# A conditional last group: one conditional with two copies of what follows, or two conditionals around the result ahead of it

## The chip, the cores and the metric

The kernel runs on one core of a Trainium2 chip. The core has a matrix engine (TensorE, here PE, with its weight loads as PEld), a vector engine (DVE), a scalar engine (ACT), GpSimd (POOL) and SyncE (SP). Each engine has a sequencer that runs its own list of instructions in order; the engines wait for each other through semaphores. In this kernel SP starts nearly all the transfers from HBM, and POOL the scatters of result rows. The metric is the device time of one execution in microseconds (us), told as the median of the runs.

## The reference

Attention in chunks, and behind it a mixture of experts with one expert per token. Cut to what is computed:

```python
# attention: B, H, S, D = 8, 8, 576, 64, in chunks of 64
scores = (1/8) * q_c @ k_c.T              # per chunk, 64 x 64
attn = softmax(scores)
x = (attn @ v_c) -> (4608, 512)           # tokens x (heads * 64)

# router: 8 experts, cosine similarity
xn, en = x / (|x| + 1e-6), emb / (|emb| + 1e-6)
logits = xn @ en.T / tau
expert = argmax(logits);  gate = max(softmax(logits))

# experts: 512 -> 1024 -> 512, each token through its own
out[t] = gate[t] * (relu(x[t] @ w1[expert[t]]) @ w2[expert[t]])
```

All in float32. How many tokens go to which expert is known only when the router has run, on the device.

## The kernel before

**Two halves.** The first half (up to about 195 us) does the attention in 36 tiles of 128 tokens, the router, and writes each token's row to a place in DRAM (`spots`) that is sorted by expert. `groups()` then counts: each expert's tokens are cut into groups of 64, an expert's last group being partly empty. `places()` works out, for every group, the row it starts at, its expert, and whether weights must be loaded. `second` is a column of `keep`, 1 on the partitions 64 to 127 and 0 below.

**Steps and pairs.** The second half goes through the groups two at a time: a step j takes one group from the front of the sorted list and one from its end, one on each half of the 128 partitions (index s = 0, 1). 36 pairs (j = 0 to 35) are always there; `LEAST` is 36. For a pair, SP loads the tokens (`load_x`, into `xin` and `spot`), DVE turns them (`turn_xb`), PE multiplies by w1 into `h`, ACT applies the relu, DVE turns the hidden values (`hT`), PE multiplies by w2 into `y_ps` (`result`, L408), ACT scales by the gate into `y` (L420), and POOL scatters 128 rows to `out` (L427). The hidden layer of pair j + 1 is computed ahead of the result of pair j, so PE has work while ACT and DVE turn the hidden values. The order is written out by hand: each engine runs its instructions as the program has them.

**Weights on condition.** `load_w2` and `load_late` issue a 2 MB transfer per half with a flag: `load_when` (L169 to L174) reads an expert number and a flag into registers of SP, and the transfer moves data only if the flag is set. `take_next` (L290) copies new w1 weights into place inside a `tc.If` when the expert changes.

**What follows the 36 pairs.** The number of groups may be odd, and there may be more than 72. `n_odd` and `n_steps` are read into registers of all five engines (L132). Then:

- If there is an odd group (`tc.If`, L1211), `step_alone(36, before_last)` does it as a step of its own with one group, that is 64 tokens. Its hidden layer comes first, then `before_last()` with the result of pair 35 and a load of w2, then its own result. This one is laid out differently: the 64 tokens fill the 128 partitions twice, once for each half of the 512 output columns, so the result is 128x256 and goes into a tile S. `at2` (L425) is the row number doubled, plus `second`, and the scatter goes to half rows of `out`. Then `more(37)`.
- Else (L1217), `load_x(39)`, `before_last()`, the loads, and `more(37)` once more.

`more(j)` is a nest: inside a `tc.If` on the number of steps (L1206) stands a `step_alone(j)` and then `more(j + 1)`, up to j = 44. So the program holds these eight steps twice, once in each branch.

**What a conditional becomes.** Every engine that takes part has a compare-and-branch. Behind the true block stands, out of line, a false block that raises the engine's semaphores by what the true block would have raised them (the make-up block), so that later waits count right. In the program before, the blocks stand in this order: the odd branch with its eight nested steps, their make-up blocks (the innermost first), the other branch with its eight steps, their make-up blocks, and the end. In the order of the instructions of the two built programs, PE has 7261 before and 6420 after, SP 2170 and 1846, DVE 2180 and 2053, ACT 1180 and 1056, POOL 1432 and 1362.

**At the end** (L1247) SP waits for all the semaphores and drains, then all five engines meet at a barrier, which POOL gathers and releases.

Of the kernel before, what the change touches and what calls it, by code (L numbers as in the profile page):

```python
# [1 line left out]

# [7 lines left out]
FP32 = mybir.dt.float32  # L10
BF16 = mybir.dt.bfloat16
I32 = mybir.dt.int32
AF = mybir.ActivationFunctionType
ALU = mybir.AluOpType
# [11 lines left out]
def kernel(  # L26
# [88 lines left out]

    n_steps = keep.tile([1, 1], I32, name="n_steps")
    n_odd = keep.tile([1, 1], I32, name="n_odd")
    second = keep.tile([P, 1], FP32, name="second")
    bp = ctx.enter_context(tc.tile_pool(name="blk", bufs=2))

    def whole(w):
# [36 lines left out]
    def load_x(j):  # L158
        rows = []
        for s in range(2 if j != LEAST else 1):  # L160
            row = number(src_row[of_step(s, j)], SPARE, ENG.SP)
            rows.append(spots[ds(row, G), :])
        load_rows(j, rows)
# [12 lines left out]
    def load_w2(j):  # L176
        for s in range(2):
            at = of_step(s, j)
            load_when(w2_sb[s][buf_of(j)], w2_rows, eblk[at], fresh[at])
# [8 lines left out]
    def load_late(j):  # L188
        for s in range(2 if j != LEAST else 1):
            at = of_step(s, j)  # L190
            load_when(next_w1[s], w1_rows, eblk[at], swap[at])
# [14 lines left out]
    def gates(j):  # L206
        for _ in gate_parts(j):
            pass
# [188 lines left out]
        swap_next()  # L397
        turn(1)

    def result(j, ps_y):  # L400
        d = mo.pop(j)
        ps = ps_y.tile([P, D], FP32, tag="y", name="y_ps")
        one_group = j == LEAST
        w = D // 2 if one_group else D
        for c in range(KF):
            for r in range(P // Q):
                t0, s, d0 = (r % 2, 0, w * (r // 2)) if one_group else (r, r // 2, 0)
                nc.tensor.matmul(  # L408
                    ps[Q * r : Q * r + Q, 0:w],
                    lhsT=d["hT"][:, c, Q * t0 : Q * t0 + Q],  # L410
                    rhs=w2_sb[s][buf_of(j)][:, c, d0 : d0 + w],
                    start=(c == 0),
                    stop=(c == KF - 1),
                )
        if one_group:
            S = late_p.tile([P, 3, KD // 2, 2, Q], FP32, tag="S", name="S", bufs=2)
            y = S.rearrange("p a c b i -> p (a c b i)")
        else:
            y = bp.tile([P, D], FP32, tag="y", name="y", bufs=1)
        nc.scalar.activation(y[:, 0:w], ps[:, 0:w], AF.Copy, scale=gate_of.pop(j))  # L420
        to, at, bound = out, spot[:, j % SPOTS, TOK : TOK + 1].bitcast(I32), N - 1
        if one_group:

            at2 = bp.tile([P, 1], I32, tag="at2", name="at2")
            nc.vector.tensor_scalar(at2, at, 2.0, second, ALU.mult, ALU.add)  # L425
            to, at, bound = out.rearrange("n (s d) -> (n s) d", s=2), at2, 2 * N - 1
        ins = nc.gpsimd.indirect_dma_start(  # L427
            out=to,
            out_offset=bass.IndirectOffsetOnAxis(ap=at, axis=0),
            in_=y[:, 0:w],  # L430
            in_offset=None,
            bounds_check=bound,
            oob_is_err=False,
        )
        tc.declare_no_dep(ins.ins, group="rows", reason="blocks hold different tokens")
        tc.add_to_no_dep_group("rows", ins.ins)
# [8 lines left out]
    with (  # L445
# [417 lines left out]
        def groups():  # L863


            half = 0.5 - 0.5 / G
            n_g = one.tile([P, E], FP32, name="n_g")
            nc.vector.tensor_scalar(
                nb[:, 1 : E + 1], rt_ps[:, 3, 0], 1.0 / G, half, ALU.mult, ALU.add
            )  # L870
            nc.vector.tensor_scalar(
                nb[:, 1 : E + 1], nb[:, 1 : E + 1], ROUND, ROUND, ALU.add, ALU.subtract
            )
            left = one.tile([P, E], FP32, name="left")
            nc.vector.tensor_tensor(left, nb[:, 1 : E + 1], done, ALU.subtract)
            nc.vector.tensor_tensor_scan(n_g, ones, left, 0.0, ALU.mult, ALU.add)
            nc.vector.tensor_scalar(off, n_g[:, E - 1 : E], -1.0, second, ALU.add, ALU.mult)
            nc.vector.tensor_tensor(first, n_g, left, ALU.subtract)
            nc.vector.tensor_scalar(mid, n_g[:, E - 1 : E], 0.5, -0.25, ALU.mult, ALU.add)
            nc.vector.tensor_scalar(mid, mid, ROUND, ROUND, ALU.add, ALU.subtract)  # L880
            nc.vector.scalar_tensor_tensor(
                out=odd, in0=mid, scalar=-2.0, in1=n_g[:, E - 1 : E], op0=ALU.mult, op1=ALU.add
            )
            nc.vector.tensor_tensor(ahead, odd, first_s, ALU.mult)


            nc.vector.tensor_scalar(
                jump[:, 0], nb[:, 0:E], -float(G), float(R), ALU.mult, ALU.add
            )
            nc.vector.scalar_tensor_tensor(  # L890
                out=jump[:, 0], in0=done, scalar=float(G), in1=jump[:, 0], op0=ALU.mult, op1=ALU.add
            )
# [234 lines left out]
    with (  # L1127
        tc.tile_pool(name="ps_h", bufs=1, space=PSUM, reuse_waits="tile") as ps_h,
        tc.tile_pool(name="ps_y", bufs=2, space=PSUM, reuse_waits="tile") as ps_y,
    ):  # L1130
        H_PS = [P, G // Q, KF * Q]

        def hidden_plain(j, w1, behind_it=None):
            for s in range(2 if j != LEAST else 1):
                ps = bank(ps_h, H_PS)
                for b in range(G // Q):
                    hidden_part(j, s, b, w1, None, None, ps)
                if behind_it is not None:
                    behind_it(s)

        def first_parts():
            for g in first_gates:
                next(g, None)

        first_parts()
        for j in range(LEAST - 1):
            n = j + 2

            def turn_next():
                if n < LEAST:  # L1150
                    turn_xb(n)
                    if n + XBUF < NJ:
                        load_x(n + XBUF)
                    add_x(n)

            def swap_next():
                if NE <= n < LEAST:
                    take_next(n)

            if j == 0:  # L1160
                first_parts()
                add_up(0, None, TS)
                first_parts()
            elif j == 1:
                turn_next()
                add_up(1, None, TS)
                hidden_plain(2, w1_sb, lambda s: add_up(s, None, ("T3",)))
            else:
                gate = gate_parts(n) if n < LEAST else iter(())
                hidden_fast(j + 1, ps_h, gate, turn_next, swap_next)  # L1170

            result(j, ps_y)
            if NE <= next_of(j) < NJ:
                load_w2(next_of(j))
            if NE - 1 <= n < LEAST - 1:
                load_behind(n)
            elif n == LEAST - 1:
                load_late(LEAST)

        steps = number(n_steps, NST, ENG.PE, ENG.DVE, ENG.Activation, ENG.Pool, ENG.SP)  # L1180

        odd_one = number(n_odd, 1, ENG.PE, ENG.DVE, ENG.Activation, ENG.Pool, ENG.SP)

        def before_last():
            result(LEAST - 1, ps_y)
            load_w2(LEAST + 1)

        def step_alone(j, between=None):
            turn_xb(j)
            if j + XBUF < NJ:  # L1190
                load_x(j + XBUF)
            gates(j)
            hidden_plain(j, next_w1)
            if j + 1 < NJ:
                load_late(j + 1)
            if between is not None:
                between()
            result(j, ps_y)
            if j + 2 < NJ:
                load_w2(j + 2)  # L1200

        def more(j):
            if j == NJ:
                return

            with tc.If(steps > j - NE - 1):  # L1206
                step_alone(j)
                more(j + 1)

        had, had_mo, had_gate = dict(xin), dict(mo), dict(gate_of)  # L1210
        with tc.If(odd_one > 0) as if_odd:  # L1211
            step_alone(LEAST, before_last)
            more(LEAST + 1)
        for now, then in ((xin, had), (mo, had_mo), (gate_of, had_gate)):
            now.clear()
            now.update(then)
        with if_odd.Else():  # L1217
            del xin[LEAST]
            load_x(LEAST + XBUF)
            before_last()  # L1220
            load_w2(LEAST + 2)
            load_late(LEAST + 1)
            more(LEAST + 1)


# [26 lines left out]
```

## Time and profile before

| what | value |
|---|---|
| time, median of 3 runs | 657.39 us (654.38 to 658.06) |
| time of the profiled execution | 657.75 us |
| its span, first to last instruction | 656.0 us |
| mean granted TensorE clock | 0.993 |
| PE, busy | 617.0 us (94%) |
| ACT, DVE, POOL, busy | 429.7, 425.3, 183.9 us |
| last matmul ends at about | 645 us |
| bytes moved by DMA, mean rate | 112.68 MB, 172 GB/s |

Times in the profile are us from the start of the span. A row of the timeline gives start, duration, engine, line, operation, what it writes and reads, the count, and in brackets how long the engine had been idle before it and what ended that. A line view gives, per engine and operation, the count, the shortest, median and longest duration in ns, and the first and last start in us; a q behind the engine's name means that its sequencer alone is at work. A row of waits gives the engine, tile and line that waited, what it waited for, the total in us, how many times, and the longest. In such a view taken branches and compares are both called COMPARE_BRANCH.

### The profile page before, as it was taken

How to read it: one execution, taken by the hardware profiler on the slowest of the kernel's cores; microseconds unless marked ns; L12 is line 12 of the kernel's file. 1: busy time of each engine (PE TensorE's matmuls, PEld its weight loads, DVE VectorE, ACT ScalarE, POOL GpSimd, SP SyncE). 2: the span in 40 equal slices, each digit the busy share in tenths (PEclk: the TensorE clock that was granted, in tenths of full speed). 3: DMA queues.
4: the chain of work that ended last, by engine and by line, in shares of the span. 5: the costliest groups of instructions: out<-in, count | busy, mean ns of one | idle time of the engine just before them, and what ended most of it. 6: DMA issues, size and time to landing. Idle time of an engine off the chain costs nothing. (4 is left out here: it accounts for less than half of the span.)

```text
span 656.0 us, 24867 instructions
## 1 busy us (share of the span) xinstructions
PE 617.0 (94%) x9744; PEld 344.5 (53%) x9744; DVE 425.3 (65%) x1140; ACT 429.7 (66%) x758; POOL 183.9 (28%) x262
## 2 busy tenths in 40 slices
PE   6899989898898989999999999999999999999993
PEld 5778878775443435445444544665444444444431
DVE  4878888786697446647784566979546666654430
ACT  4767767674316757767676767776777777676650
POOL 7759897762410100003020002303010021000101
PEclk9999999999998999999999999999999999999998
DMA  9999999988528711112787111776821116311111
GB/s 259 302 253 276 275 293 283 333 280 299 220 64 304 285 41 40 46 39 72 285 316 265 53 44 43 292 302 236 341 62 44 47 39 217 129 39 35 51 32 36
DMA packets 91696, 112.68 MB, mean 172 GB/s; under 512 B 49260, under 2 KB 69484, under 8 KB 91560
## 3 DMA queue, kind: packets, MB, share of 16 engines
q1 hardware_dynamic: 79512, 71.99, 34.0%
q0 software_dynamic: 12016, 38.89, 17.5%
q8 instruction: 81, 1.33, 0.8%
q14 instruction: 55, 0.45, 0.2%
q10 hardware_dynamic: 32, 0.02, 0.0%
HBM read 334.71 MB, written 22.69 MB: 545 GB/s over the span
## 5 line engine op out<-in xcount | busy, mean ns | idle before, releaser
L408 PE MATMUL y_ps<-w,hT 128*32 128x512 f32 (+1 forms) x2368 | 278.0, 587 | 2.9 <-DMA w<-in_moe_w_dram 2.9
L356 ACT ACTIVATE h<-C 64x256 f32<-64x256 f32 x264 | 179.4, 679 | 69.9 <-DVE C L369 67.1
L408 PEld LDWEIGHTS y_ps<-w,hT 128*32 128x32 f32 x2368 | 91.2, 110 | 155.4 <-issue 136.0
L427 POOL DMA_INDIRECT out_dram<-y,spot x36 | 37.5, 1042 | 392.4 <-ACT y L420 301.6
L337 PE MATMUL h<-w,S 128*32 128x256 f32 x1056 | 108.4, 382 | 1.8 <-DVE w L286 1.8
L337 PE MATMUL h<-sums,xbT 128*32 128x256 f32 x1056 | 109.0, 383 | 0.5 <-DVEq L294 0.5
L369 DVE TENSOR_TENSOR C<-C,h 128x256 f32<-128x256 f32 x231 | 96.0, 416 | 11.2 <-PE h L337 4.4
L363 DVE STREAM_TRANSPOSE hT<-h 128x512 f32<-128x512 f32 x66 | 46.7, 708 | 55.2 <-ACT h L356 54.5
L337 PE MATMUL h<-w,xbT 128*32 128x256 f32 x1056 | 82.3, 379 | 0.0
L222 DVE TENSOR_SCALAR rn<-rn 128x1 f32<-128x1 f32 x37 | 5.6, 151 | 87.6 <-ACT rn L219 87.6
L337 PEld LDWEIGHTS h<-w,S 128*32 128x32 f32 x1056 | 49.3, 110 | 24.2 <-DVE w L286 1.5
L337 PEld LDWEIGHTS h<-sums,xbT 128*32 128x32 f32 x1056 | 49.4, 111 | 23.2 <-DVEq L294 1.4
L337 PEld LDWEIGHTS h<-w,xbT 128*32 128x32 f32 x1056 | 43.6, 110 | 31.6 <-issue 9.0
L420 ACT ACTIVATE y<-y_ps,gate 128x512 f32<-128x512 f32 x36 | 24.8, 688 | 50.6 <-issue 44.7
L337 PE MATMUL h<-sums,S 128*32 128x256 f32 x528 | 53.4, 379 | 0.0
L816 POOL DMA_INDIRECT spots<-xr,dest x36 | 37.4, 1039 | 28.0 <-DVE dest L781 9.8
L198 DVE STREAM_TRANSPOSE xbT<-xin 128x256 f32<-128x256 f32 x73 | 44.4, 646 | 0.5 <-DVE hT L363 0.5
L219 ACT ACT_TABLE_LOAD x34 | 43.6, 1283 | 0.9 <-issue 0.4
L226 ACT ACT_TABLE_LOAD x34 | 43.6, 1283 | 0.6
L698 ACT COPY xT<-tr 128x512 f32<-128x512 f32 x36 | 21.1, 586 | 32.3 <-PE tr L696 32.3
L586 POOL DMA_DIRECT2D kx<-in_k_dram x36 | 31.9, 888 | 13.4 <-PE tr L612 12.6
L586 POOL DMA_DIRECT2D qx<-in_q_dram x40 | 34.5, 865 | 0.7 <-PE tr L612 0.6
(204 smaller groups left out, 802.2 us busy)
## 6 DMA issues: line engine op xcount, KB each, us to landing
w<-in_moe_w_dram SPq DMA_DIRECT2D x74, 2048.0 KB
next_w<-in_moe_w_dram SPq DMA_DIRECT2D x67, 2048.0 KB
xin<-spots SPq DMA_DIRECT2D x158, 64.0 KB
qx<-in_q_dram POOLq DMA_DIRECT2D x32, 256.0 KB, 5.9
v<-in_v_dram SPq DMA_DIRECT2D x58, 128.0 KB
kx<-in_k_dram POOLq DMA_DIRECT2D x28, 256.0 KB, 4.6
spots<-blank SPq DMA_DIRECT2D x9, 144.0 KB
spot<-spots SPq DMA_DIRECT2D x80, 4.0 KB
```

The costliest lines, as they stand in the source:

```text
L198: nc.vector.transpose(xT[:, :, cols].rearrange("p c (b i) -> p b c i", i=Q), t[:, s * (D // 2) : (s + 1) * (D // 2)].rearrange("p (b i c) ...
L219: nc.scalar.activation(rn, spot[:, j % SPOTS, SQ : SQ + 1], AF.Sqrt)
L226: nc.scalar.activation(sh, sh, AF.Exp, accum_out=gate)
L337: nc.tensor.matmul(ps[t0 : t0 + Q], lhsT=a[:, c, s], rhs=w[:, r], start=c == 0, stop=c == KD // 2 - 1,)
L356: nc.scalar.activation(h[b][G * v : G * v + G, s].rearrange("p (k i) -> p k i", i=Q), x[G * s : G * s + G].rearrange("p (i k) -> p k i", i=Q),
L363: nc.vector.transpose(hT.rearrange("p k (s b i) -> p b s k i", b=2, i=Q)[:, b], h[b].rearrange("p s (k i) -> p s k i", i=Q),)
L369: nc.vector.tensor_tensor(out, a, b, op)
L408: nc.tensor.matmul(ps[Q * r : Q * r + Q, 0:w], lhsT=d["hT"][:, c, Q * t0 : Q * t0 + Q], rhs=w2_sb[s][buf_of(j)][:, c, d0 : d0 + w], start= ...
L420: nc.scalar.activation(y[:, 0:w], ps[:, 0:w], AF.Copy, scale=gate_of.pop(j))
L427: ins = nc.gpsimd.indirect_dma_start(out=to, out_offset=bass.IndirectOffsetOnAxis(ap=at, axis=0), in_=y[:, 0:w], in_offset=None, bounds_ch ...
L586: eng.dma_start(out=x[done : done + n], in_=src[b, :, s : s + n, :].rearrange("h p d -> p h d"),)
L816: ins = nc.gpsimd.indirect_dma_start(out=spots, out_offset=bass.IndirectOffsetOnAxis(ap=at, axis=0), in_=m, in_offset=None, bounds_check=S ...
```

## The change

The conditional on the odd group becomes two, with the result of pair 35 between them and outside of both.

- First conditional: `turn_xb`, `gates` and the hidden layer of step 36.
- Outside: `load_x(39)`, a tile S that POOL sets to zero, the result of pair 35, `load_w2(37)`, `load_late(37)`.
- Second conditional: the matmuls of step 36's result and its scaling into S (`scaled`).
- Outside: `at2` and the scatter of S, then `load_w2(38)` and `more(37)`, which is now written once.

Since the scatter runs also when there is no odd group, `half_row` replaces `second` in `at2`: for an even count it is larger by 2N, which puts every row number out of bounds, and the scatter drops such rows. It is worked out in `groups()` by two more DVE operations. `second` and `half_row` are two columns of one tile. `result` is split into `scaled` and `scatter`, with the conditional as an argument.

```diff
-    second = keep.tile([P, 1], FP32, name="second")
+    by_half = keep.tile([P, 2], FP32, name="by_half")
+    second, half_row = by_half[:, 0:1], by_half[:, 1:2]
...
-    def result(j, ps_y):
+    def result(j, ps_y, y=None, when=nullcontext):
+        if y is None:
+            y = bp.tile([P, D], FP32, tag="y", name="y", bufs=1)
+        with when():
+            scaled(j, ps_y, y)
+        scatter(j, y)
+
+    def scaled(j, ps_y, y):
         d = mo.pop(j)
...
-        if one_group:
-            S = late_p.tile([P, 3, KD // 2, 2, Q], FP32, tag="S", name="S", bufs=2)
-            y = S.rearrange("p a c b i -> p (a c b i)")
-        else:
-            y = bp.tile([P, D], FP32, tag="y", name="y", bufs=1)
-        nc.scalar.activation(y[:, 0:w], ps[:, 0:w], AF.Copy, scale=gate_of.pop(j))
+        nc.scalar.activation(y, ps[:, 0:w], AF.Copy, scale=gate_of.pop(j))
+
+    def scatter(j, y):
         to, at, bound = out, spot[:, j % SPOTS, TOK : TOK + 1].bitcast(I32), N - 1
-        if one_group:
+        if j == LEAST:
             at2 = bp.tile([P, 1], I32, tag="at2", name="at2")
-            nc.vector.tensor_scalar(at2, at, 2.0, second, ALU.mult, ALU.add)
+            nc.vector.tensor_scalar(at2, at, 2.0, half_row, ALU.mult, ALU.add)
...
             nc.vector.tensor_tensor(ahead, odd, first_s, ALU.mult)
+            nc.vector.tensor_scalar(half_row, odd, -2.0 * N, 2.0 * N, ALU.mult, ALU.add)
+            nc.vector.tensor_tensor(half_row, half_row, second, ALU.add)
...
-        had, had_mo, had_gate = dict(xin), dict(mo), dict(gate_of)
-        with tc.If(odd_one > 0) as if_odd:
-            step_alone(LEAST, before_last)
-            more(LEAST + 1)
-        for now, then in ((xin, had), (mo, had_mo), (gate_of, had_gate)):
-            now.clear()
-            now.update(then)
-        with if_odd.Else():
-            del xin[LEAST]
-            load_x(LEAST + XBUF)
-            before_last()
-            load_w2(LEAST + 2)
-            load_late(LEAST + 1)
-            more(LEAST + 1)
+        def when_odd():
+            return tc.If(odd_one > 0)
+
+        with when_odd():
+            turn_xb(LEAST)
+            gates(LEAST)
+            hidden_plain(LEAST, next_w1)
+        load_x(LEAST + XBUF)
+        S = late_p.tile([P, 3, KD // 2, 2, Q], FP32, tag="S", name="S", bufs=2)
+        y_odd = S.rearrange("p a c b i -> p (a c b i)")[:, 0 : D // 2]
+        nc.gpsimd.memset(y_odd, 0.0)
+        result(LEAST - 1, ps_y)
+        load_w2(LEAST + 1)
+        load_late(LEAST + 1)
+        result(LEAST, ps_y, y_odd, when_odd)
+        load_w2(LEAST + 2)
+        more(LEAST + 1)
```

More of the change, by code (lines that the diff above doesn't have):

```diff
@@ L1 @@
-from contextlib import ExitStack
+from contextlib import ExitStack, nullcontext
 import concourse.bass as bass
@@ L429, in result @@
             out_offset=bass.IndirectOffsetOnAxis(ap=at, axis=0),
-            in_=y[:, 0:w],
+            in_=y,
             in_offset=None,
@@ L1182, with step_alone @@
         odd_one = number(n_odd, 1, ENG.PE, ENG.DVE, ENG.Activation, ENG.Pool, ENG.SP)
[L1184 to L1188, printed above, removed]
+        def step_alone(j):
             turn_xb(j)
@@ L1195, in step_alone @@
                 load_late(j + 1)
-            if between is not None:
-                between()
             result(j, ps_y)
```

## The prediction

> **What bounds the kernel now.** I read the page's busy times first, then the stretch that the diff touches (the timeline from 641 us), then, because little engine work is left there, the sequencers' own records of the lines that branch and end the program (line views, which give count, shortest, median and longest duration in ns, and first and last start).
>
> ```profile
> PE 617.0 (94%) x9744; PEld 344.5 (53%) x9744; DVE 425.3 (65%) x1140; ACT 429.7 (66%) x758; POOL 183.9 (28%) x262
> ```
>
> PE sets the pace to 645 us. Everything that the diff edits at the end stands in the last 27 us; of the 656.0 us span, the last 11 have no matmul. The timeline there:
>
> ```profile
> 641.66 0.69 ACT L420 ACTIVATE y<-y_ps,gate 128x512 f32<-128x512 f32 x1 [5.62 <-issue]
> 642.61 4.05 SPq L172 DMA_DIRECT2D w<-in_moe_w_dram  x4
> 642.63 0.97 POOL L427 DMA_INDIRECT out_dram<-y,spot  x1 [9.35 <-ACT y L420]
> 645.07 0.47 ACT L420 ACTIVATE S<-y_ps,gate 128x256 f32<-128x256 f32 x1 [2.72 <-PE y_ps L408]
> 645.82 0.97 POOL L427 DMA_INDIRECT out_dram<-S,at  x1 [2.22 <-ACTq L1206]
> ```
>
> Two readings decide much. First, the half-width result into S runs: **with these inputs there is an odd group**, so the kernel before takes the first of its two copies, and no further step follows. The second copy, which the change deletes, costs no time now. Second, the order at the end is PE, then ACT 645.07 to 645.54, then the scatter at 645.82. What comes after it is seen in the sequencers alone:
>
> ```profile
> L1206 SPq EVENT_SEMAPHORE  x9: 17/17/17, 650.3 to 650.9; - x9
> L1206 PEldq COMPARE_BRANCH  x2: 3417/3983/4549, 643.3 to 647.0; - x2
> L1206 SPq COMPARE_BRANCH  x2: 38/44/50, 646.7 to 651.0; - x2
> L1206 POOLq EVENT_SEMAPHORE  x2: 43/43/43, 646.8 to 650.0; - x2
> L1206 POOLq INC_SWDGE_SEM  x1: 1026/1026/1026, 650.1 to 650.1; - x1
> L1206 POOLq COMPARE_BRANCH  x1: 38/38/38, 651.1 to 651.1; - x1
> ```
>
> ```profile
> L1247 SPq EVENT_SEMAPHORE  x12: 28/28/28, 653.7 to 654.4; - x12
> L1247 SPq DRAIN  x2: 7/10/13, 654.4 to 654.5; - x2
> ...
> L1247 POOLq DRAIN  x1: 3591/3591/3591, 651.5 to 651.5; - x1
> ```
>
> When "steps > 32" is false, each engine jumps past eight nested steps to a small block that makes up the semaphores, and from there past the whole second copy to the program's end. SP branches at 646.7 and its next instruction starts at 650.3 (3.6 us); it branches again at 651.0 and goes on at 653.7 (2.7 us). PE's two far jumps last 3.4 and 4.5 us. **Two chains end the span**: SP's (jump, 9 semaphores, jump, 12 semaphores, drain at 654.5) and POOL's (the scatter's landing, which lets it go on at 650.0; 1.0 us for the counters; a drain from 651.5 to 655.1). POOL's is later by 0.6 us, and from 655.1 a barrier of 0.9 us closes the span.
>
> **The change part by part.**
>
> *The deleted copy.* It isn't executed. What it gives is distance: the make-up block now stands directly ahead of the end, so the second far jump goes. Worth 2.6 us on SP, 4.5 on PE, but only as far as the end waits for them; POOL's own second jump takes 0.4 us (651.1 to 651.5), so on POOL at most 0.3.
>
> *Two more conditional edges on each engine.* When the first conditional is true, its block now ends in a jump over a make-up block of one semaphore instruction, and the second has a compare, a true block and such a jump. The nearest rows are the same construct inside the loop, which jumps over the weight copies when no expert changes:
>
> ```profile
> L294 POOLq COMPARE_BRANCH  x2: 45/45/45, 606.8 to 607.6; - x2
> L294 POOLq EVENT_SEMAPHORE  x2: 17/17/17, 607.0 to 607.8; - x2
> ```
>
> Near jumps: branch at 606.8, target at 607.0, that is 0.2 us. Two jumps and a compare come to about 0.5 us per engine. On POOL they lie in the idle time ahead of the two scatters (9.35 and 2.22 us in the timeline), on ACT in 5.62 and 2.72 us, on DVE behind its last work. On PE no near jump is to be seen, so I bound it: from below by that 0.2 us, from above by the far 3.4. PE's sequencer runs ahead of its array:
>
> ```profile
> L1211 PEldq COMPARE_BRANCH  x1: 92/92/92, 629.1 to 629.1; - x1
> ```
>
> This branch was done at 629.2, while the result matmuls ahead of it end at 631.2 in the timeline, and the last far branch was taken at 643.3 with matmuls until 645.0: 1.7 to 2.0 us of cover. 0.2 us costs nothing; 3.4 would leave up to 1.7 us bare ahead of the last pair's result, and ACT's result and the scatter would be late by it. The second jump on PE comes after its last matmul and delays nobody but its own sequencer. I take 0, as the target is three instructions away and the far targets are over a thousand.
>
> Here a rule speaks against the change. The Trainium skill, "Runtime: NRT & Kernel Launch", section "Instruction fetch mechanics", has a taken branch stall for a fetch when its target is outside the buffered window, which for most engines is two blocks of 256 instructions. If the two new jumps on SP each cost such a fetch, that is 2 x 2.6 to 2 x 3.6 = 5 to 7 us; by the row of L294 it is 0.4. Targets two to four instructions away are inside the window by that rule also, unless a block's edge falls between. I take the row. The rule explains the far rows: the second jump passes some 330 instructions on SP (stall) and 78 on POOL (0.4 us, none).
>
> *SP's order.* Same twelve transfers issued, in another order: the loads of pair 37's w2 now stand ahead of its w1. In the timeline the conditional loads move nothing that matters (the last slices of the page show 32 to 51 GB/s), but SP issues one in about 1.25 us (four from 642.61 to 646.66). w2 must wait until pair 35's result matmuls end, when ACT starts at 641.66; before, the two w1 loads were issued in that time, the first at 640.08. Now: first w2 at 641.6, then 642.8, w1 at 644.1 and 645.4, two edges 0.4, last two w2 at 647.0 and 648.2, branch at 648.3 instead of 646.7: 1.6 later. Plus far jump 3.6 = 651.9, 9 semaphores 0.7, and no second jump but 0.2: 652.8; 12 semaphores and drain 0.8: 653.6. Against 654.5 SP is earlier by 0.9 and stays behind nobody: 1.5 us of slack to POOL. The x loads, now outside the conditional, keep their place.
>
> *POOL and ACT at the end.* POOL has a memset of S (128x256), between the scatters of 34 and 35. Its buffer is free since pair 34's products (about 611 us), and it lies in the 9.35 us of idle time; the 0.16 us memset of 128x40 at 181 us is the nearest row, and even 1 us is covered. Behind the memset stands the scatter of 35, which waits for ACT until 642.6. at2 on DVE moves behind two edges: DVE's last work ends near 637, the address is needed at 645.5. The result into S must now also wait for the memset, so one semaphore instruction more stands in front of it on ACT and on POOL: 0.05 to 0.1 each on the path, I take **+0.1** (0 to 0.3).
>
> *Scatter always, out of bounds when even.* Here odd, so it sends the same rows: 0.
>
> *Two more DVE operations in groups(),* of one element per partition, in the routing stage:
>
> ```profile
> 173.71 0.16 DVE L881 SCALAR_TENSOR_TENSOR odd<-mid,n_g 128x1 f32<-128x1 f32 x1
> 173.91 0.16 DVE L884 TENSOR_TENSOR ahead<-odd,first_s 128x1 f32<-128x1 f32 x1
> ```
>
> ```profile
> PE h L337 <- DVE w L286: 1.8, 2, 1.0
> ```
>
> Dependent ones follow each other at 0.20 us; one of the two can overlap: 0.3 to 0.4. PE is busy meanwhile, but DVE has hardly an idle moment from there to 202 us, where PE waits twice for its T3 sums (second view: PE's waits from 196 to 204 us). So it comes through: **+0.35** (0 if the wait of 2.6 us for w2 at 232 us swallows it, as its transfer is issued earlier or not).
>
> **Sum:** 0.35 + 0.1 + 0 on PE + 0 in POOL's drain = +0.45 us on the profiled execution: 656.0 becomes 656.5 in span, 657.75 (1.75 lie around the span) becomes 658.2. That execution stands 0.36 above the median of 657.39, so I forecast **657.8**, +0.07%. The three runs spread over 3.7 us; 0.5% or 3.3 us is about what can be told from no change.
>
> **The rivals.**
>
> *A, near jumps on SP cost a fetch.* For it: SP is the engine with the longest make-up blocks, and every jump of it seen here stalled; no near one is seen. Against it: 0.2 us on POOL and 0.2 on DVE for the same construct, all through the loop. SP's drain at 653.6 + 5.3 to 7.2 = 658.9 to 660.8, against POOL's 655.1: +3.8 to 5.7, with 0.45 it gives 661.6 to 663.5. It decides once the two together exceed SP's slack of 1.5 us. Slower.
>
> *B, POOL's drain is part of the second jump.* For it: this drain takes 3.6 us where the two behind it take 0.1 and less, and it begins just after the jump. Against it: it starts 0.4 us after the branch, so the instruction was there. Without it SP's 653.6 ends the chain: -1.5, with 0.45 about 656.3.
>
> *C, SP's tail keeps its second stall,* because a block's edge falls among its 25 closing instructions, or PE's near jump isn't covered. SP's drain at 653.6 + 2.6 = 656.2, +1.1 over POOL; PE: +1.7. With 0.45: 658.9 to 659.5.
>
> *That the change does nothing it names here* is the likeliest case itself: the deleted copy never ran.
>
> **How the numbers follow.** Likeliest 0.62 (its own range 656.6 to 658.8, the median's scatter), B 0.14, C 0.14, A 0.10. B and C stay within 3.3 us, A doesn't, and with drift between measurements I give faster 0.04, same 0.86, slower 0.10. The range reaches from B less 0.7 of scatter to C's upper end plus 0.5: 655.6 to 660.1.
>
> **What would show it.** No gap between the matmuls of pair 36's hidden layer and pair 35's result; the S scatter about 0.5 us after its old place; SP's last issues near 648; one far gap on SP instead of two, its drain a good us before POOL's; POOL's drain still over 3 us. Wrong if SP shows gaps of microseconds behind the new branches, if PE idles there, or if POOL's drain shrinks.

## The result

The changed kernel took **658.13 us** (median of 14 executions, 656.73 to 663.78), the kernel before 657.87 us in the same comparison (14 executions, 654.38 to 661.41). The ratio is **1.0018, with a 95% interval of 0.9997 to 1.0040**: no change that this measurement can tell. A second comparison on another chip gave 658.01 against 656.81 us, ratio 1.0033 (1.0015 to 1.0051). So if there is a difference, it is a loss of some 0.2%, about 1 us; the forecast was 657.8 us, +0.07%.

The profiled execution of the changed kernel took 656.73 us, with a span of 655.0 us and a mean granted TensorE clock of 0.986 (0.993 before). Its busy times, from the page:

```profile
PE 618.1 (94%) x9744; PEld 354.7 (54%) x9744; DVE 425.9 (65%) x1142; ACT 429.6 (66%) x758; POOL 184.7 (28%) x263
```

The same number of matmuls, two operations more on DVE, one more on POOL (the memset): the deleted copy had done nothing with these inputs. The timeline of the changed kernel from 641.5 us, PE left out:

```profile
641.59 1.35 SPq L173 DMA_DIRECT2D w<-in_moe_w_dram  x2
642.07 0.69 ACT L423 ACTIVATE y<-y_ps,gate 128x512 f32<-128x512 f32 x1 [5.63 <-issue]
643.03 0.98 POOL L432 DMA_INDIRECT out_dram<-y,spot  x1 [8.98 <-ACT y L423]
644.07 1.55 SPq L173 DMA_DIRECT2D next_w<-in_moe_w_dram  x2
645.52 0.47 ACT L423 ACTIVATE S<-y_ps,gate 128x256 f32<-128x256 f32 x1 [2.77 <-PE y_ps L416]
646.76 0.97 POOL L432 DMA_INDIRECT out_dram<-S,at  x1 [2.75 <-ACTq L1207]
647.09 1.27 SPq L173 DMA_DIRECT2D w<-in_moe_w_dram  x2
```

SP's six loads stand where the prediction put them (641.6, 644.1, 647.0 for the first of each two). But the scatter of S starts 0.77 us after ACT is done (645.52 + 0.47 = 645.99, then 646.76); before it was 0.28 us. The sequencers, from the line views of the nest's conditional (L1207), of the end (L1251) and of the new second conditional (L404):

```profile
L1207 SPq EVENT_SEMAPHORE  x9: 17/17/17, 651.0 to 651.6; - x9
L1207 PEldq COMPARE_BRANCH  x1: 4135/4135/4135, 644.0 to 644.0; - x1
L1207 SPq COMPARE_BRANCH  x1: 50/50/50, 648.4 to 648.4; - x1
L1207 POOLq INC_SWDGE_SEM  x1: 1026/1026/1026, 649.4 to 649.4; - x1
...
L1251 POOLq DRAIN  x3: 46/103/3507, 650.4 to 654.5; - x3
L1251 SPq DRAIN  x3: 7/7/13, 652.4 to 654.2; - x3
...
L404 ACTq COMPARE_BRANCH  x2: 38/38/39, 642.1 to 645.5; - x2
L404 SPq COMPARE_BRANCH  x2: 34/36/38, 645.7 to 645.7; - x2
L404 PEldq COMPARE_BRANCH  x1: 174/174/174, 643.7 to 643.7; - x1
```

One far jump on each engine in place of two: PE's lasts 4.1 us, SP's 2.6 (648.4 to 651.0). The near jumps cost nothing that shows: 174 ns on PE, and SP's next instruction starts at 645.92, 0.17 us after its jump (of its two rows at L404 the first is the compare, the second, 0.08 us later, the jump). POOL still ends the span, with the drain of 3.5 us, and SP drains 1.5 us ahead of it.

One row differs in an unexpected way. Before, the scatter of S was issued at 645.82 and POOL went on at 650.0; now it is issued at 646.76 and POOL goes on at 649.3. The wait's end stands in the sequencer's records at 649.96 and 649.26: **the landing took 4.14 us before and 2.50 us after**. The prediction had held it for the scatter's own price. That is where this tail got shorter, from 10.95 to 9.53 us behind the last matmul, although the scatter starts later. Of these 1.4 us the span shows 1.0 (656.0 to 655.0), as pair 34's scaling began 0.4 us later (631.75 against 631.35). What shortened the landing was the first question.

A stretch that can be compared among all executions, on whatever chip, is the one from the start of ACT's scaling of pair 34 (the last that comes ahead of everything edited) to the end of the span: 24.62 us before (631.35 to 655.97), 23.21 after. The middle, from pair 4's scaling to pair 34's, is 388.2 us in both.

### The profile page after: what moved, and what is told of

Its sections match the earlier page's. It is cut to its first block, busy times and chain, and to the rows that moved or that the text cites. A ratio compares the mean times of both kernels' runs of the same rounds, so it can differ in the third digit from the quotient of the medians.

```text
span 655.0 us, 24884 instructions
## 1 busy us (share of the span) xinstructions
PE 618.1 (94%) x9744; PEld 354.7 (54%) x9744; DVE 425.9 (65%) x1142; ACT 429.6 (66%) x758; POOL 184.7 (28%) x263
## 3 DMA queue, kind: packets, MB, share of 16 engines
q8 instruction: 79, 1.29, 0.8%
## 5 line engine op out<-in xcount | busy, mean ns | idle before, releaser
L416 PEld LDWEIGHTS y_ps<-w,hT 128*32 128x32 f32 x2368 | 103.2, 110 | 145.1 <-issue 91.9
L338 PE MATMUL h<-w,S 128*32 128x256 f32 x1056 | 102.4, 379 | 2.1 <-DVE w L287 2.1
L338 PE MATMUL h<-sums,xbT 128*32 128x256 f32 x1056 | 102.5, 379 | 0.6 <-DVEq L295 0.6
L338 PE MATMUL h<-w,xbT 128*32 128x256 f32 x1056 | 79.5, 379 | 0.0
L338 PEld LDWEIGHTS h<-w,xbT 128*32 128x32 f32 x1056 | 42.0, 110 | 32.3 <-issue 6.6
L338 PE MATMUL h<-sums,S 128*32 128x256 f32 x528 | 50.8, 379 | 0.0
```

The source lines that it names most:

```text
L338: nc.tensor.matmul(ps[t0 : t0 + Q], lhsT=a[:, c, s], rhs=w[:, r], start=c == 0, stop=c == KD // 2 - 1,)
L416: nc.tensor.matmul(ps[Q * r : Q * r + Q, 0:w], lhsT=d["hT"][:, c, Q * t0 : Q * t0 + Q], rhs=w2_sb[s][buf_of(j)][:, c, d0 : d0 + w], start= ...
```

## The experiments

On three of the chips the kernel before took 664 to 669 us, the excess being in the first 190 us; so single executions are compared in the stretches that the edits touch. "Tail" is the time from pair 34's scaling to the end of the span.

**The kernel before, once more.** No edit.

> The kernel before once more, for a second trace of its end. Theory L (code fetches of the second far jumps, on PE and SP, share the DMA engines with the last scatter and slow its landing): from the start of the S scatter to POOL's next semaphore 4.2 us again (645.8 to 650.0 in the first trace). Rival (landing differs from execution to execution): anything from 2.5 to 4.2. POOL's drain 3.5 to 3.6 us in either case.

Measured: 671.09 us, tail 23.16. Timeline, and line views of L1206 and L1247:

```profile
659.78 0.47 ACT L420 ACTIVATE S<-y_ps,gate 128x256 f32<-128x256 f32 x1 [2.72 <-PE y_ps L408]
660.53 0.97 POOL L427 DMA_INDIRECT out_dram<-S,at  x1 [2.22 <-ACTq L1206]
...
L1206 PEldq COMPARE_BRANCH  x2: 4107/4470/4834, 658.0 to 662.3; - x2
L1206 SPq COMPARE_BRANCH  x2: 38/44/50, 661.4 to 664.8; - x2
...
L1247 POOLq DRAIN  x3: 46/103/3591, 664.7 to 668.9; - x3
L1247 SPq DRAIN  x3: 7/7/13, 668.3 to 668.6; - x3
```

Both far jumps are there, and yet the landing took 2.60 us (to 663.13). So the second far jump doesn't always make the landing longer; the run with the late front, below, comes back to it. Also, with a short landing, POOL's drain ends at 668.30 (664.71 + 3.59) and SP's begins at 668.33: **the two chains end together**, where the prediction had seen 0.6 us between them.

**The deleted copy alone.** The kernel before without its second branch (so it leaves out the even case); the first conditional is as it was, with no memset and no scatter outside.

```diff
-        for now, then in ((xin, had), (mo, had_mo), (gate_of, had_gate)):
-            now.clear()
-            now.update(then)
-        with if_odd.Else():
-            del xin[LEAST]
-            load_x(LEAST + XBUF)
-            before_last()
-            load_w2(LEAST + 2)
-            load_late(LEAST + 1)
-            more(LEAST + 1)
```

> Before, without its Else branch: with these inputs it never runs, so only the distance to the program's end changes; an even count of groups is left out. Theory L: one far jump on SP and PE instead of two, landing of the S scatter 2.5 us instead of 4.2, POOL's chain and the end earlier by about 1.7 us after the last matmul (9.3 instead of 10.9 us). Rival (landing by chance): SP's drain earlier by 2.4, POOL's unchanged, 10.9 us after the last matmul. ACT's end to the scatter stays 0.27 us.

Measured: 669.14 us, tail 22.74, landing 2.59. Line views of L1206 and of the end (L1237):

```profile
L1206 PEldq COMPARE_BRANCH  x2: 193/2142/4090, 656.2 to 660.5; - x2
L1206 SPq COMPARE_BRANCH  x2: 38/44/50, 659.6 to 662.9; - x2
...
L1237 POOLq DRAIN  x3: 46/103/3507, 662.7 to 666.7; - x3
L1237 SPq DRAIN  x3: 7/7/13, 663.9 to 666.4; - x3
```

The second jump is near now: 0.19 us on PE in place of 4.83. SP's drain comes 2.7 us sooner, counted from its first branch (659.65 to 663.85, against 661.43 to 668.33). The tail shrinks by 0.42 us only, because POOL ends it: its second jump goes from 0.40 to 0.15 us and its drain from 3.59 to 3.51. So with landings of the same length, and by one execution of each, the whole worth of the deleted copy in the odd case is **0.4 us**.

**The memset on another engine.** The changed kernel with one line different.

```diff
-        nc.gpsimd.memset(y_odd, 0.0)
+        nc.vector.memset(y_odd, 0.0)
```

> After, with the zeros of S written by DVE and not by POOL. Theory W (the new wait for POOL's own memset takes the place on the scatter instruction, and the wait for ACT moves into a semaphore instruction ahead of it, so that the scatter is prepared only when ACT is done): from ACT's end to the scatter's start 0.27 us as before, not the 0.77 of after. Rival E (the new edges on POOL and ACT cost it): 0.77 stays. Rest of the end as in after: 2.5 us landing, drain 3.5.

Measured: 667.70 us, tail 22.38, landing 2.39. Timeline:

```profile
657.26 0.47 ACT L423 ACTIVATE S<-y_ps,gate 128x256 f32<-128x256 f32 x1 [2.71 <-PE y_ps L416]
658.01 0.97 POOL L432 DMA_INDIRECT out_dram<-S,at  x1 [2.22 <-ACTq L1207]
```

657.73 to 658.01: **0.28 us again**, with both conditional edges still there. So the 0.49 us come from the wait, not from the edges. In the changed kernel the scatter has two waits, on ACT and on POOL's own memset. In the sequencer's records the one on the memset, long fulfilled, sits on the scatter instruction itself, and the one on ACT in a semaphore instruction ahead of it, which must first end. Without the memset the order is the other way about: what comes last is waited for on the scatter. The same in every execution: 0.76 to 0.78 us with the memset on POOL (the changed kernel twice, and the next one), 0.27 or 0.28 in all three with it on DVE.

**Without the eight nested steps.** The changed kernel without its last line. It leaves out the steps beyond pair 36, which these inputs don't take.

```diff
-        more(LEAST + 1)
```

> After, without the eight further steps; with these inputs none of them runs, more than 73 groups are left out. No far jump, no make-up of the scatters' counters on POOL. If POOL's 3.5 us drain belongs to that make-up (1.0 us instruction, its work going on behind it), it shrinks to 0.1 and the span ends about 4.5 us earlier against the last matmul (5 instead of 9.5 us). If the drain stands by itself, it stays 3.5 and only 1.0 us goes. PE's and SP's last instructions come 3 to 4 us earlier either way.

Measured: 667.73 us, tail 20.81, landing 2.38. Timeline and the end's line view (L1250):

```profile
660.16 0.97 POOL L432 DMA_INDIRECT out_dram<-S,at  x1 [2.76 <-ACT S L423]
...
L1250 POOLq DRAIN  x3: 109/193/4710, 659.9 to 665.5; - x3
L1250 SPq DRAIN  x3: 7/7/13, 663.1 to 664.9; - x3
```

With no make-up of counters, POOL's drain is issued while the scatter still runs, and ends at 664.64: 3.51 us after the scatter's 0.97 us end (661.13). In every other execution it starts behind the make-up and lasts 3.43 to 3.59 us. So it is a **fixed 3.5 us after POOL's last work**; it is no part of a jump, and it doesn't wait for the landing (662.54), beside which it runs here. The make-up block costs more than its 1.03 us: it waits for the landing and so puts landing and drain one behind the other, 2.3 to 2.4 us of the tail.

**A late front.** The kernel before with 21 dependent operations of 128x1 on DVE where the change has two.

```diff
             nc.vector.tensor_tensor(ahead, odd, first_s, ALU.mult)
+            nc.vector.tensor_scalar(lim, ahead, 0.0, None, ALU.mult)
+            for _ in range(19):
+                nc.vector.tensor_scalar(lim, lim, 0.0, None, ALU.mult)
+            nc.vector.tensor_tensor(ahead, ahead, lim, ALU.add)
```

> The kernel before with 21 dependent operations of 128x1 more on VectorE in the counting of groups, at the place where the change has its two (0.2 us each, 4.2 us in all; they add zero to the number that is used next). Theory D (as predicted: VectorE's chain sets when PE gets its T3 sums, 0.35 of the two operations' 0.4 us comes through): PE's waits for the T3 sums near 200 us, together 0.4 to 1.8 us before, become 4.2 us longer. Behind them stands PE's wait for the w2 transfer near 232 to 249 us. Theory S (the transfer's time does not depend on PE): that wait shrinks to nothing, and of 4.2 us only what exceeds it (4.2 less 0.3 to 4.7) reaches the end: +0 to +3.9 us. Theory P (the transfer is issued later by as much): the wait stays what it was, and the whole +4.2 us (0.64%) reaches the end.

Measured: ratio 1.0040 (1.0007 to 1.0073), that is +2.7 us with an interval of 0.5 to 4.9, which doesn't tell the theories apart. The trace does. The timeline of this kernel, DVE's counting and SP's first load of w2, and PE's wait for w2:

```profile
184.85 0.16 DVE L881 SCALAR_TENSOR_TENSOR odd<-mid,n_g 128x1 f32<-128x1 f32 x1
210.09 2.03 SPq L172 DMA_DIRECT2D w<-in_moe_w_dram  x2
...
PE y_ps L408 <- DMA w<-in_moe_w_dram: 4.5, 1, 4.5
```

The same rows of the kernel before (its wait for w2 is the one that the prediction speaks of), and of the changed kernel:

```profile
173.71 0.16 DVE L881 SCALAR_TENSOR_TENSOR odd<-mid,n_g 128x1 f32<-128x1 f32 x1
194.97 2.03 SPq L172 DMA_DIRECT2D w<-in_moe_w_dram  x2
...
PE y_ps L408 <- DMA w<-in_moe_w_dram: 2.6, 1, 2.6
```

```profile
171.92 0.16 DVE L886 SCALAR_TENSOR_TENSOR odd<-mid,n_g 128x1 f32<-128x1 f32 x1
193.46 2.03 SPq L173 DMA_DIRECT2D w<-in_moe_w_dram  x2
...
PE h L338 <- DVE w L287: 2.1, 2, 1.1
...
PE y_ps L416 <- DMA w<-in_moe_w_dram: 4.7, 1, 4.7
```

From `odd` to the load it is 21.26 us before, 21.54 in the changed kernel and 25.24 here: **+0.28 for the two operations, +3.98 for the 21.** The other executions agree: 21.25 to 21.27 in three more without the two operations (a fourth had 23.44, and why was not found out), 21.49 to 21.55 in all eight with them. So w2 can't swallow the delay, since its transfer is itself issued after the routing; theory S falls, P holds. From `odd` to pair 4's scaling it is 74.45 us here and 68.55 to 71.39 in the five others without added operations. The wait for the T3 sums came to 2.6 us in place of the 4.6 to 6.0 expected: against the 0.4 of the kernel before in its second execution it grew by 2.2 and not by 4.2. Why was not found out; the load is late by nearly the whole chain all the same.

This execution, meant for the front, has the tail of the kernel before as well: both far jumps, tail 25.27 us, and a landing of **4.79 us**. So of three executions with that tail two have a long landing (4.14, 4.79) and one a short one (2.60); of the seven with an odd group whose second jump is gone, none (2.38 to 2.59). What holds a long landing up, the trace's records of the single transfers say. The kernel before, the DMA view of the 1.4 us in which the long landing ends (row DMA: busy share in 40 slices of 0.035 us):

```profile
DMA  0000080009000000000000000006000000000000
...
q0 software_dynamic: 3, 0.01, 4.3%
q14 instruction: 1, 0.01, 2.1%
```

All that is left of the scatter is three packets. The others were through by 647.85. These wait: the first starts at 648.53, and a transfer of 16 KB of instructions (queue q8) ran from 647.46 to 648.58. With the late front it is the same to 0.05 us: instructions 663.98 to 665.65, the last packets of the scatter from 665.62. Where the landing is short, that transfer starts when the scatter's packets are through or, at the earliest, 0.1 us before the last of them ends. That the packets stand behind the instructions in one engine's queue is inferred from the times; the records don't name the engine, and don't say whose jump a transfer serves.

Is it the second far jump's transfer? By the times it need not be. PE's second jump was taken at 647.01, but a 16 KB transfer also comes where there is no such jump. The DMA view of 661.05 to 661.20 us of the run without the second branch, and of 648.70 to 648.80 in the changed kernel:

```profile
q8 instruction: 1, 0.02, 49.4%
```

```profile
q8 instruction: 1, 0.02, 56.7%
```

In all nine executions with an odd group and the nest one starts 0.66 to 0.84 us after the end of PE's *first* far jump, and that jump stays in the changed kernel. In us after the start of the scatter of S, whose packets run from 1.55 to about 2.05 where nothing holds them up:

| execution | second far jump | first far jump ends | 16 KB transfer starts | landing |
|---|---|---|---|---|
| before | yes | 0.91 | 1.64 | 4.14 |
| before, late front | yes | 0.90 | 1.67 | 4.79 |
| before, once more | yes | 1.60 | 2.35 | 2.60 |
| before without the second branch | no | 1.58 | 2.36 | 2.59 |
| changed, twice | no | 1.32, 1.35 | 1.98, 2.02 | 2.50, 2.38 |
| changed, memset on DVE, three | no | 1.81 to 1.91 | 2.58 to 2.65 | 2.38 to 2.39 |

The landing is long where the transfer starts among the packets, and that was so where the first jump was short (3.4 us in the two executions with a long landing, 4.1 to 4.2 in the others). The scatter ahead, that of pair 35, shows the same without any second jump: in the run without the second branch a 16 KB transfer starts 1.61 us after it and it lands after 4.73 us; in the run without the nested steps there is no far jump and no instruction transfer, and it lands after 2.71. The second jump may add to a long landing, as a further 16 KB transfer starts 1.0 to 1.2 us after it in all three, but no run has a first jump that ends 0.9 us after the scatter and no second one. So whether the deleted copy makes the landing of S long, or the length of the first jump does that alone, is open; the times speak for the first jump.

**The even case.** These inputs have an odd group, so the deleted copy never runs. To see it run, both kernels got a condition that is never true; the odd group is left out of the result. In the changed kernel the scatter of S still sends its rows, zeros, since `half_row` follows the true count; so its dropping of rows in a truly even case was not run.

```diff
-        odd_one = number(n_odd, 1, ENG.PE, ENG.DVE, ENG.Activation, ENG.Pool, ENG.SP)
+        odd_one = number(n_odd, 2, ENG.PE, ENG.DVE, ENG.Activation, ENG.Pool, ENG.SP)
...
-        with tc.If(odd_one > 0) as if_odd:
+        with tc.If(odd_one > 1) as if_odd:
```

(and the same in `when_odd` of the changed kernel)

> The kernel before, with the condition on the odd group asking for more than one, which is never true: the odd group is left out, and every engine takes the copy of the tail that the change deletes. Theory F (a taken jump stalls by its distance): PE's jump at the first conditional passes the whole odd branch with its eight nested steps, far over a thousand instructions, so it stalls for 3.4 to 4.5 us as the two far jumps of the profile of before did. It is taken about 2 us ahead of the end of pair 34's result, so PE's array stands still for 1.5 to 3 us ahead of the result of pair 35. After that result one far jump, a make-up block and the end: SP one gap of 2.5 to 3.6 us. Theory C (PE's sequencer covers it): the array shows no gap there over 0.5 us.

> The changed kernel with both conditions on the odd group asking for more than one, never true: the odd group's matmuls are left out, the result of pair 35 follows in place. Theory F: the first jump passes 64 matmuls and their weight loads alone, lasts 0.2 us on PE and is covered, so the array goes from pair 34's result to pair 35's with less than 0.5 us of gap; the last matmul comes 1.5 to 3 us sooner, counted from the end of pair 34's result, than in the other kernel of this pair. Against it: if 128 instructions of distance already leave the fetched window, PE stalls 3.4 us or more here too, and the gap is the same as in the other. In either case the closing drain of GpSimd is 3.5 us from the make-up of its counters (1.03 us) as it was with the odd group.

Measured: 668.81 us, tail 23.22, and 662.88 us, tail 20.63. The rest of the 6 us between them lies ahead of pair 34. Timeline of PE and line views, first of the kernel before with its condition never true, then of the changed one:

```profile
645.60 7.07 PE L408 MATMUL y_ps<-w,hT 128*32 128x512 f32 x64 [1.89 <-DVEq L1206]
...
L1211 PEldq COMPARE_BRANCH  x1: 3864/3864/3864, 641.6 to 641.6; - x1
L1211 SPq COMPARE_BRANCH  x1: 50/50/50, 645.5 to 645.5; - x1
...
L1247 SPq DRAIN  x3: 7/7/13, 666.1 to 666.5; - x3
```

```profile
640.60 7.07 PE L416 MATMUL y_ps<-w,hT 128*32 128x512 f32 x64 [0.31 <-PEq L1214]
...
L1214 PEldq COMPARE_BRANCH  x1: 375/375/375, 638.2 to 638.2; - x1
L1214 SPq COMPARE_BRANCH  x1: 50/50/50, 642.1 to 642.1; - x1
...
L1251 SPq DRAIN  x3: 7/7/13, 659.9 to 660.3; - x3
```

Theory F holds: a jump past eight nested steps stalls PE for 3.9 us, of which 1.9 show as a gap; one past 64 matmuls and their weight loads takes 0.38 us. But it is SP that ends both spans (its drain at 666.1 and 659.9, POOL's ending at 662.4 and 657.4). There the far jump took 3.4 us (645.5 to the next instruction at 648.9), the near one 0.2, and all the loads stand behind it. So the tail's 2.6 us come from SP's jump, 3.2 us shorter, of which 0.6 are lost again on the way (0.2 of it by the second conditional's edge), and PE's 1.6 are covered.

The same two, timed:

> The kernel before with its first condition never true, so that the odd group is left out and the copy that the change deletes runs. Less work than the kernel before by the odd group's 4.2 us of matmuls for the hidden layer and 3.4 for the result, plus the idle 1.9 us on TensorE and SyncE's later tail (13.5 us behind the last matmul and not 9.5): about -2 us, 0.3%.

> The changed kernel with both conditions never true, so that the odd group is left out. By the traces of one execution each, the stretch from the end of pair 34's result to the end of the span is 20.7 us here and 23.3 us in the other one: 2.6 us less, plus 0.28 for the two operations on VectorE: 2.3 us or 0.35% under the kernel before with its condition never true. The rival, that the two executions differ by what lies ahead of pair 35 (which was 3.4 us apart for no reason in the code), says the same time to 0.1%.

Against the kernel before: 0.9993 (0.9968 to 1.0018) and 0.9984 (0.9963 to 1.0005), medians 656.33 and 656.10 us. The traces repeat (tails 23.21 and 20.60 us), but the medians are 0.2 us apart and not 2.3. That is a miss, though with intervals of 1.6 us to each side 2.3 us is at the edge of what could be told; where the tail's gain went is not known.

**The changed kernel and the DVE memset, timed.**

> The changed kernel again, as the measure for the next one. Sum of the traces: +0.28 us by the two operations on VectorE, +0.49 by the scatter that waits for its own memset, about -0.4 by the second far jump of SyncE where that engine ends last: +0.3 to +0.4 us, 0.05%, not to be told from no change. The rival that the change is worth something after all by the shorter program says -0.3% or more.

> The changed kernel with the memset of S on VectorE in place of GpSimd. Theory W (the wait's place costs 0.49 us): 0.4 to 0.5 us under the changed kernel, 0.07%, and level with the kernel before to 0.1 us. An interval of 0.3% can't show it; it can show a loss, if VectorE's memset were late for anything (that theory says +0.3% or more).

Ratios 1.0033 (1.0015 to 1.0051) and 0.9992 (0.9969 to 1.0015), medians 658.01 and 655.62 us; tails 23.10 and 22.37. Between the two lie 2.4 us, of which the tails hold 0.7. So the second was measured again, on another chip:

> The changed kernel with the memset on VectorE once more, on another day's chip perhaps. In the last timing it was 0.08% under the kernel before and the changed kernel 0.33% over it: 2.4 us between the two, where the traces' tails hold 0.7 us (9.42 and 8.70 us behind the last matmul). If the 1.7 us in excess are chance, the ratio to the kernel before now lies nearer to 1.000 to 1.002, since the two operations on VectorE (+0.28 us) and the far jump saved (-0.4 us) all but cancel. If they are real, it is 0.998 to 0.999 again.

Ratio 0.9999 (0.9967 to 1.0031), tail 22.37. This is the value for chance, though the interval excludes neither. The version with the memset on DVE is the best of the three by its tail (22.4 us in three executions; changed kernel 23.1 and 23.2; before 23.2, 24.6 and, with the late front, 25.3), and level with the kernel before in time. No version was measured to be faster.

## Why the prediction was right, and where its steps were not

- *The deleted copy costs nothing now.* Right: same matmuls, and the bound by SP and POOL was right in kind. With a short landing it is worth 0.42 us (copy alone deleted), where the prediction had "at most 0.3" on POOL and put 0 into its sum.
- *The landing.* Here a reading was wrong. The 4.1 us between the scatter and POOL's next instruction were taken as fixed; undisturbed they are 2.4 to 2.6, and the profile before was one of the two executions in which an instruction transfer held the last packets up. With a short landing the slack of 0.6 us between SP's chain and POOL's is gone. That PE's second jump "delays nobody but its own sequencer" is neither shown nor refuted, as the transfer that was in the way fits the first jump as well.
- *One semaphore instruction more, +0.1 us (0 to 0.3).* Right kind, wrong size: 0.49 us, outside the bounds. What costs is not the extra instruction but that the last wait moved off the scatter.
- *Near jumps.* Right: 0.17 us on PE, covered; rival A (a fetch for each near jump on SP) falls, as SP goes on 0.17 us after its own. The row of L294 was the right one to take. The section "Instruction fetch mechanics" of the Trainium skill ("Runtime: NRT & Kernel Launch") held as well: past 64 matmuls and their weight loads PE took 0.34 to 0.38 us, past the nested steps or the second copy 3.4 to 4.9. Of the instruction transfers, those of queue q8 are 16 KB, the block that the page states; those of q14 are 8 KB (79 of 1.29 MB and 49 of 0.40 MB on the changed kernel's page).
- *SP's order.* Issues at 641.6, 644.1 and 647.1 against 641.6, 644.1 and 647.0; branch at 648.4 against 648.3. The far jump took 2.6 us and not 3.6, so the drain came at 652.4 and not 653.6. Rival C falls with it.
- *POOL's drain.* Rival B falls: 3.5 us without the second jump, and even without the nest.
- *Two DVE operations, +0.35 us.* 0.28 by the load's issue (0.3 by the waits for T3, 1.8 to 2.1). The doubt whether w2's wait swallows them is settled: it doesn't.

With landings of the same length the traces make it 0.28 + 0.49 - 0.42 = +0.35 us in place of +0.45. The tails agree: 23.16 us before with a short landing, 23.21 and 23.10 for the changed kernel, so the later scatter and the deleted copy cancel there. That the sum came so close is in part luck: the prediction put 0.1 where 0.49 was measured, and 0 where -0.42 was. If one takes the mean of all three tails before instead (24.35), the changed kernel gains 1.2 us there and the sum becomes 0.28 - 1.2 = -0.9, but that rests on the two long landings, which can't be put down to the change.

The two timings say +0.3 and +1.2 us by their medians. From `odd` to pair 4 the eight executions with the two operations took 69.9 to 72.4 us, mean 71.0, the five others without the long chain 68.6 to 71.4, mean 70.1; the spread within each group is larger than that difference and hides whether anything of it is the change's. Whether the changed kernel is slower by a microsecond or so is therefore open: the two intervals reach from -0.2 to +2.6 and from +1.0 to +3.3 us.

## What to carry to other kernels

A branch that is not taken is free only in busy time: what it puts between a jump and its target was paid here as a stall of 2.4 to 4.9 us on SP and PE, and an instruction transfer can delay a store that is just landing. When an instruction gets a second wait, look in the sequencer's records which of the two stands on the instruction and which ahead of it: the one that comes last should be on it. And a wait in the tail is to be seen in more than one execution before its length is booked as the price of the instruction that it waits for, and a cause that fits the executions with the long wait is to be looked for in those with the short one too.

## What was not expected of the hardware

- The same 128-row scatter lands in 2.4 to 2.6 us or in 4.1 to 4.8, depending on whether a 16 KB instruction transfer starts while its packets run (1.64 and 1.67 us after the scatter) or behind them (1.98 to 2.65).
- POOL's closing drain lasts 3.43 to 3.59 us after its last work, whether or not the scatter has landed.
- A scatter starts 0.27 us after ACT ends when it waits for ACT itself, 0.77 us when the wait stands in an instruction ahead of it.
- The same far jump takes 2.7 to 3.6 us on SP and 3.4 to 4.1 on PE in different executions of the same kernel; over all runs far jumps take 2.4 to 3.6 us on SP and 3.4 to 4.9 on PE. A 16 KB instruction transfer follows the end of each of PE's within 0.9 us.
